# The output product of a gated MLP, taken for pairs of token tiles: seven block products in place of eight

## The chip, the core and the metric

The kernel runs on one core of one Trainium2 chip. The metric is the device time of one execution in microseconds. The program is one launch; nothing is computed on the host but the layout of the inputs.

The engines are named as in the profile: PE multiplies matrices (PEld is its loading of weights), DVE is the vector engine, ACT the scalar engine, POOL the general one, SP issues the DMAs. Matmul results land in banks of PSUM of 128 partitions x 512 float32 numbers, which DVE and ACT read. All other tiles are in SBUF.

## The reference

The input `x` has 2048 tokens of 512 numbers. It goes through a block of linear attention and then through a gated MLP, each behind a layer norm and a modulation by a condition `c`. Only the MLP matters here:

```python
z = gelu(h @ w_in)                    # h: 2048 x 512, z: 2048 x 1376
z1 = z[..., :688]
z2 = layernorm(z[..., 688:])
g = w_sp @ z2 + b_sp[:, None]         # w_sp: 2048 x 2048, mixes tokens
x = x + gb * ((z1 * g) @ w_out)       # w_out: 688 x 512
```

The change is in the last line: u = z1 * g, and u @ w_out with the gate `gb` already multiplied into `w_out`.

## The kernel before

Tokens lie in 16 tiles of 128, features on the free axis. Precision is kept by splitting each float32 operand into a high part, the copy to `fp32r` that ACT makes, and a low part, the rest, that DVE (sometimes POOL) subtracts. A product takes three matmuls, hi x hi, hi x lo and lo x hi, added up in one bank.

The program's order is written out by hand in lists of two-letter steps with arguments (`ORDER` for the first part, `ORDER3` for the rest); `run_all` emits them one after the other. Each engine, and SP for the DMAs, runs its own instructions strictly in this order; waits between engines come from the tiles that the steps write and read. `SLOTS` gives, tag by tag, the buffer number that each new tile takes: a tile's first write waits until the last reader of the tile before it in that buffer is done. `st` has 4 buffers of 4 KB a partition (raw pieces of `w_sp`, later the tiles `ur`), `s4` has 8, `md` 4, `zs` 16, `tq` 24.

`ORDER` does the attention and most of z. In `ORDER3` come, in this order:

- the token mixing g = w_sp @ z2. It is done for pairs of token tiles p = 0 to 7. The step `pr` is one of seven block products of a pair (pair 0 is done plainly by `pp`); `ss`, `fh`, `fl` and `fg` prepare the blocks of `w_sp`, and `cs`, `cd` and `ce` collect the banks P into u on DVE and ACT;
- for each tile t: `um` multiplies u by z1 (loaded by `lz`), `up` splits the words into two planes of 16 bits on ACT, `ux` transposes them by a DMA, `ug` merges them on ACT, `uq` parks the transposed u in DRAM. A transposed tile has six blocks of 128 columns: five with features 0 to 639, and a sixth whose partitions 0 to 47 and again 64 to 111 hold the last 48 features, so that one matmul over 112 partitions adds two of the three parts;
- the output product, PE's last stage. `ow`, `om`, `oh` and `os` load w_out in six blocks, multiply each by the gate and split it. For each tile, `ur` brings u back from DRAM into `st`, `uh` copies its high part on ACT (two instructions), `ul` makes the low part on DVE (three: L1039, L1041, L1042), `wm` does 17 matmuls into one bank `pout` (five blocks x 3, and 2 for the sixth), `ot` (L1086) adds the bank to the tile `x3` (loaded by `lx`) on DVE and stores it. The last tile is done in two halves of 256 columns, in two banks.

```python
PO[t, c0] = bank((t + (c0 > 0) + 7) % 8, f"pout{t}_{c0}")
...
mm3(p, v[:, 0], v[:, 1], WO[k][:, 0, c0:c1], WO[k][:, 1, c0:c1], k == 0, False)
```

Of the kernel before, what the change touches and what calls it, by code (L numbers as in the profile page):

```python
# [26 lines left out]
def block_kernel(ctx: ExitStack, tc: tile.TileContext, x, x_t, w_qkv, w_o, w_in, w_sp, b_sp, w_out,  # L27
# [3 lines left out]
    def pool(name, bufs, space=None, stack=None):  # L31
        if space is None:
# [28 lines left out]
        "tb": (
            "251640514236030560456512032560032302036043413024561031352613565461602135052644561533456312004154"
            "234246531320450302120102222300635564150423"
        ),
        "s4": (
            "106302405147035246037134521305131465713675741303537526703524167402671536504370142376454076531264"
            "315024517360017374267103627044167154073167540267503612751046237452601464563274610370567512037423"
            "20510673161562547073065123024513452134"
        ),
# [951 lines left out]
    UR = {}

    def u_back(t):
        UR[t] = sb("st", [P, 768], F32, f"ur{t}")
        dma(UR[t], UD[t])

# [159 lines left out]
```

## Time and profile before

| what | us |
|---|---|
| median of 3 runs | 617.71 (616.91 to 618.66) |
| the profiled execution's own time | 616.95 |
| its span, first to last instruction | 615.0 |
| busy in the span: PE | 608.7 |
| DVE | 464.2 |
| ACT | 362.2 |
| POOL | 212.2 |

The span is what the profile shows; the profiled execution took 1.95 us more. An engine is busy while it has an instruction in it, so PE's busy time tells that it is nearly always fed, not that it is at its peak. A line number is one of the kernel before; a helper such as `mm3` (L110 to L112) stands for all who call it, so tiles tell the stages apart: `pout<-wout,ut` is the output product. "x<-x,pout" is the output add, "ut<-ur,ut" the low part of u.

### The profile page before, as it was taken

The page shows a single profiled execution, that of the slowest core. Times are in us where ns is not written, and L with a number is a line of the kernel's source. Part 1 is how long each engine was busy: PE and PEld are TensorE (multiplying, and loading weights), DVE is VectorE, ACT ScalarE, POOL GpSimd, SP SyncE. Part 2 cuts the span into 40 slices and gives each one's busy share as a digit, 9 for nine tenths or more (in the row PEclk, how much of TensorE's full clock was granted, in tenths as well). Part 3 has the DMA queues.
Part 4 walks back from the last instruction along what each step waited for, and adds up shares of the span by engine and source line. Part 5 has one row for each costly group of instructions (what it writes and reads, how often), then busy time and mean ns, then how long its engine had stood idle before and what let it go on. Part 6 is the DMA issues. An engine that isn't in the chain of part 4 may idle for free.

```text
span 615.0 us, 9440 instructions
## 1 busy us (share of the span) xinstructions
PE 608.7 (99%) x3359; PEld 555.6 (90%) x3359; DVE 464.2 (75%) x873; ACT 362.2 (59%) x619; POOL 212.2 (34%) x180
## 2 busy tenths in 40 slices
...
GB/s 303 126 179 98 122 118 44 147 165 40 87 109 120 185 147 192 136 170 260 274 59 326 270 148 169 126 195 101 192 208 129 229 140 175 196 243 284 311 239 113
DMA packets 91022, 105.74 MB, mean 172 GB/s; under 512 B 57088, under 2 KB 57600, under 8 KB 90976
## 3 DMA queue, kind: packets, MB, share of 16 engines
...
q8 instruction: 26, 0.43, 0.3%
q14 instruction: 20, 0.16, 0.1%
...
## 4 chain that ended last, share of the span: by engine, by line
PE 84%; DVE 7%; ACT 3%; DMA 3%; POOL 1%; issue 1%; SPq 1%; ACTq 0%; DVEq 0%; POOLq 0%
PE P L944 30%; PE z L654 13%; PE Pq L944 5%; PE z L860 2%; PE g L112 2%; PE g L110 2%; PE pout L112 2%; PE g L111 2%; PE pout L110 2%; PE pout L111 2%; PE qp L111 2%; PE qp L110 2%; PE qp L112 2%; PE kp L110 2%; PE kp L111 2%; PE kp L112 2%
## 5 line engine op out<-in xcount | busy, mean ns | idle before, releaser
L944 PE MATMUL P<-z,f 128*128 128x344 f32 x672 | 109.8, 320 | 0.0
L654 PE MATMUL z<-win,ht 128*128 128x344 f32 x672 | 107.9, 320 | 0.2 <-ACT z L659 0.2
L654 PEld LDWEIGHTS z<-win,ht 128*128 128x128 f32 x672 | 106.4, 188 | 1.3 <-ACT z L659 0.5
L944 PEld LDWEIGHTS P<-z,f 128*128 128x128 f32 x672 | 106.6, 188 | 0.0
L934 POOL TENSOR_TENSOR f<-raw_wsp,f 128x512 fp32r<-128x512 f32 x28 | 39.6, 1423 | 172.7 <-ACT f L931 150.2
L254 POOL TENSOR_TENSOR mv<-ve,mhalf 128x1 f32<-128x1 f32 x48 | 35.2, 736 | 68.3 <-DVE nm L387 34.4
L931 ACT ACTIVATE f<-raw_wsp 128x512 fp32r<-128x512 f32 x56 | 34.2, 626 | 37.2 <-PE P L944 20.3
L934 DVE TENSOR_TENSOR f<-sa,f 128x512 fp32r<-128x512 f32 x42 | 32.0, 769 | 18.5 <-ACT f L931 16.5
L931 ACT ACTIVATE f<-sa 128x512 fp32r<-128x512 f32 x42 | 25.8, 625 | 20.6 <-issue 8.4
L278 ACT COPY uca<-ucb 128x768 uint16<-128x768 uint16 x32 | 31.9, 1063 | 7.0 <-DMA ucb<-uca 6.9
L112 PE MATMUL pout<-wout,ut 128*128 128x512 f32 (+1 forms) x85 | 32.3, 380 | 0.7 <-DVE ut L1039 0.7
L110 PE MATMUL pout<-wout,ut 128*128 128x512 f32 (+1 forms) x85 | 32.5, 383 | 0.0
L111 PE MATMUL pout<-wout,ut 128*128 128x512 f32 (+1 forms) x85 | 32.2, 379 | 0.0
L1033 ACT ACTIVATE ut<-ur 128x384 fp32r<-128x384 f32 x32 | 15.6, 519 | 27.9 <-DMA ur<-ud 11.0
L944 PE MATMUL Pq<-z,wsp 128*128 128x344 f32 x192 | 31.0, 321 | 0.0
L944 PEld LDWEIGHTS Pq<-z,wsp 128*128 128x128 f32 x192 | 30.6, 188 | 0.0
L476 POOL TENSOR_TENSOR pksum<-pksum,tk 128x512 f32<-128x512 f32 x15 | 22.3, 1486 | 18.0 <-DVE tk L448 14.5
L268 ACT COPY uca<-us 128x768 uint16<-128x768 uint16 x32 | 24.9, 826 | 5.2 <-PE P L944 2.0
L583 POOL TENSOR_TENSOR prod<-pq,zrep 128x512 f32<-128x512 f32 x16 | 21.8, 1376 | 15.7 <-DVE den L591 5.0
L934 DVE TENSOR_TENSOR f<-raw_wsp,f 128x512 fp32r<-128x512 f32 x28 | 19.8, 714 | 8.3 <-ACT f L931 8.3
L112 PE MATMUL po<-m,pt 128*128 128x512 f32 x64 | 25.4, 397 | 0.1
L110 PE MATMUL po<-m,pt 128*128 128x512 f32 x64 | 25.4, 396 | 0.0
(254 smaller groups left out, 1546.4 us busy)
## 6 DMA issues: line engine op xcount, KB each, us to landing
...
```

The source lines that it names most:

```text
L110: mm(o, a_hi, b_hi, start=first, stop=False, **kw)
L111: mm(o, a_hi, b_lo, start=False, stop=False, **kw)
L112: mm(o, a_lo, b_hi, start=False, stop=last, **kw)
L254: nc.gpsimd.tensor_tensor(mv[:, 1:2], ve, mhalf, op=OP.pow)
L268: nc.scalar.copy(pl[:, h], v[:, :, h])
L278: copy(o[:, :, h], plt[:, h * n:(h + 1) * n].rearrange("p a b -> p (a b)"))
L476: nc.gpsimd.tensor_add(pksum, pksum, PK[t])
L583: nc.gpsimd.tensor_mul(pr, PQ[t], KV["z"])
L654: mm(p[:, b, :HB], a[:, i, kc], win[h][:, j, kc, b * HB:(b + 1) * HB], start=kc == 0 and k == 0, stop=kc == KC - 1 and k == 2)
L931: nc.scalar.activation(SF[p, h, k][:, 0], s_src(p, h, k), AF.Copy)
L934: eng.tensor_sub(SF[p, h, k][:, 1], s_src(p, h, k), f(SF[p, h, k][:, 0]))
L944: mm(B[key][:, :HB], a[:, x_], b[:, y_], start=i == 1, stop=i == n)
```

## The change

The features 0 to 511 of u and all 512 columns of w_out are cut in blocks of 256, and two token tiles 2p and 2p+1 are taken together. With A11, A12 the two feature blocks of tile 2p, A21, A22 those of tile 2p+1, and B11 to B22 the blocks of w_out, the product of 2 x 2 blocks is formed from seven block products in place of eight (Winograd's form). Each product is 128 tokens x 256 features x 256 columns, so 2 x 3 matmuls of 256 columns. The other 176 features (blocks 4 and 5 of the transposed tile) are multiplied as before, in 256-column halves.

New steps: `ua` forms one of four sums of blocks of u in place in the returned tiles (DVE, 256 wide); `uH` and `uL` split the fourth, which needs a buffer of its own in `tq`; `wa` forms one of four sums of blocks of w_out (DVE); `op` is one block product, `or` one remaining half; `oa` adds a bank, or half of one, to `x3` (DVE). The tile `ur` grows from 768 to 1024 columns, so `uh` and `ul` cover 4 blocks a half instead of 3. w_out has nine split forms instead of six.

A pair has two banks. Half 0 of the first collects the products 1, 6, 7 and 4, one after the other; between them `oa` reads what is there, since M1, M1+M6 and M1+M6+M7 are needed by other blocks of the output. Its half 1 takes the rest of tile 2p+1. The second bank collects product 2 and the rest in one half, 5, 3 and the rest in the other.

Both orders and all of `SLOTS` are written anew. `ORDER` holds the same 836 steps in another sequence. `ORDER3` differs by the new steps too. Below stand the functions, the lines of the old order with most of `wm`, and the end of the new order.

```diff
-    UR = {}
+    UR, U4 = {}, {}
 
     def u_back(t):
-        UR[t] = sb("st", [P, 768], F32, f"ur{t}")
-        dma(UR[t], UD[t])
+        UR[t] = sb("st", [P, 1024], F32, f"ur{t}")
+        dma(UR[t][:, 256:], UD[t])
+
+    def u_sum(p, k):
+        a, b = UR[2 * p], UR[2 * p + 1]
+        a11, a12, a21, a22 = a[:, 256:512], a[:, 512:768], b[:, 256:512], b[:, 512:768]
+        if k == 3:
+            nc.vector.tensor_sub(a[:, :256], a11, a21)
+        elif k == 1:
+            nc.vector.tensor_add(a21, a21, a22)
+        elif k == 2:
+            nc.vector.tensor_sub(b[:, :256], a21, a11)
+        else:
+            nc.vector.tensor_sub(b[:, :256], a12, b[:, :256])
 
     def u_word(t, n):
-        return UR[t].rearrange("p (a b) -> p a b", b=P)[:, 3 * n:3 * n + 3]
+        return UR[t].rearrange("p (a b) -> p a b", b=P)[:, 4 * n:4 * n + 4]
 
     def u_hi(t):
         for n in range(2):
-            UT[t, n] = sb("s4", [P, 2, 3, P], F32R, f"ut{n}_{t}")
+            UT[t, n] = sb("s4", [P, 2, 4, P], F32R, f"ut{n}_{t}")
             nc.scalar.activation(UT[t, n][:, 0], u_word(t, n), AF.Copy)
 
     def u_lo(t):
@@ -1038,13 +1053,39 @@
             if n == 0:
                 nc.vector.tensor_sub(o[:, 1], v, f(o[:, 0]))
             else:
-                nc.vector.tensor_sub(o[:, 1, :2], v[:, :2], f(o[:, 0, :2]))
-                nc.vector.tensor_sub(o[64:112, 0, 2], v[64:112, 2], f(o[64:112, 0, 2]))
-
-    WO = {}
+                nc.vector.tensor_sub(o[:, 1, :3], v[:, :3], f(o[:, 0, :3]))
+                nc.vector.tensor_sub(o[64:112, 0, 3], v[64:112, 3], f(o[64:112, 0, 3]))
+
+    def u4_src(p):
+        return u_word(2 * p + 1, 0)[:, :2]
+
+    def u4_hi(p):
+        U4[p] = sb("tq", [P, 2, 2, P], F32R, f"u4_{p}")
+        nc.scalar.activation(U4[p][:, 0], u4_src(p), AF.Copy)
+
+    def u4_lo(p):
+        nc.vector.tensor_sub(U4[p][:, 1], u4_src(p), f(U4[p][:, 0]))
+
+    def u_form(p, k, i):
+        if k == 3:
+            return U4[p][:, :, i]
+        a, b = 2 * p, 2 * p + 1
+        t, n = {1: (a, 0), 2: (a, 2), 4: (b, 2), 5: (b, 0), 6: (b, -2), 7: (a, -2)}[k]
+        n += 2 + i
+        return UT[t, n // 4][:, :, n % 4]
+
+    def u_rest(t, k):
+        return UT[t, 1][:, :, k - 2]
+
+    WR, WO = {}, {}
 
     def load_wout(k):
-        r = RAW["wout", k] = sb("md", [P, D], F32, f"wor{k}")
+        if k < 4:
+            if k % 2 == 0:
+                WR[k // 2] = sb("st", [P, 2, D], F32, f"wor{k}")
+            dma(WR[k // 2][:, k % 2], w_out[k])
+            return
+        r = WR[k] = sb("md", [P, D], F32, f"wor{k}")
         if k < 5:
             dma(r, w_out[k])
         else:
@@ -1053,38 +1094,80 @@
             dma(r[64:112, :], w_out_tail)
 
     def wout_mul(k):
-        r = RAW["wout", k]
-        nc.vector.tensor_mul(r, r, MOD[5])
+        r = WR[k]
+        if k < 2:
+            nc.vector.tensor_mul(r, r, MOD[5][:, None, :].to_broadcast([P, 2, D]))
+        else:
+            nc.vector.tensor_mul(r, r, MOD[5])
+
+    def wout_sum(k):
+        b11, b12, b21, b22 = WR[0][:, :, :256], WR[0][:, :, 256:], WR[1][:, :, :256], WR[1][:, :, 256:]
+        if k == 1:
+            WR["t1"] = sb("md", [P, 2, 256], F32, "wt1")
+            nc.vector.tensor_sub(WR["t1"], b12, b11)
+        elif k == 2:
+            WR["t2"] = sb("md", [P, 2, 256], F32, "wt2")
+            nc.vector.tensor_sub(WR["t2"], b22, WR["t1"])
+        elif k == 3:
+            nc.vector.tensor_sub(b12, b22, b12)
+        else:
+            nc.vector.tensor_sub(WR["t2"], b21, WR["t2"])
+
+    def w_form(k):
+        return {1: lambda: WR[0][:, :, :256], 2: lambda: WR[1][:, :, :256], 3: lambda: WR[1][:, :, 256:],
+                4: lambda: WR["t2"], 5: lambda: WR["t1"], 6: lambda: WR["t2"], 7: lambda: WR[0][:, :, 256:],
+                8: lambda: WR[4].rearrange("p (a b) -> p a b", b=256),
+                9: lambda: WR[5].rearrange("p (a b) -> p a b", b=256)}[k]()
 
     def wout_hi(k):
-        WO[k] = sb("zs", [P, 2, D], F32R, f"wout{k}")
-        nc.scalar.activation(WO[k][:, 0], RAW["wout", k], AF.Copy)
+        WO[k] = sb("zs", [P, 2, 2, 256], F32R, f"wout{k}")
+        nc.scalar.activation(WO[k][:, 0], w_form(k), AF.Copy)
 
     def wout_lo(k):
-        nc.vector.tensor_sub(WO[k][:, 1], RAW.pop(("wout", k)), f(WO[k][:, 0]))
-        if k == 5:
-            nc.gpsimd.memset(f(WO[k][64:P, 1, :]), 0.0)
+        nc.vector.tensor_sub(WO[k][:, 1], w_form(k), f(WO[k][:, 0]))
+        if k == 9:
+            nc.gpsimd.memset(f(WO[9][64:P, 1]), 0.0)
 
     def load_x3(t):
         X3[t] = sb("tq", [P, D], F32, f"x3_{t}")
         dma(X3[t], X1D[t])
 
-    PO = {}
-
-    def wout_mm(t, c0=0, c1=D):
-        PO[t, c0] = bank((t + (c0 > 0) + 7) % 8, f"pout{t}_{c0}")
-        p = PO[t, c0][:, c0:c1]
-        for k in range(5):
-            v = UT[t, k // 3][:, :, k % 3]
-            mm3(p, v[:, 0], v[:, 1], WO[k][:, 0, c0:c1], WO[k][:, 1, c0:c1], k == 0, False)
-        v = UT[t, 1][:112, 0, 2]
-        mm(p, v, WO[5][:112, 0, c0:c1], start=False, stop=False)
-        mm(p, v, WO[5][:112, 1, c0:c1], start=False, stop=True)
-
-    def out_store(t, c0=0, c1=D):
-        o = X3[t][:, c0:c1]
-        nc.vector.tensor_add(o, o, PO[t, c0][:, c0:c1])
-        dma(out[t * P:(t + 1) * P, c0:c1], o)
+    PO, NPO = {}, {}
+
+    def o_bank(p, b, c):
+        if (p, b) not in PO:
+            PO[p, b] = bank((2 * p + 7 + b) % 8, f"pout{p}_{b}")
+        return PO[p, b][:, 256 * c:256 * c + 256]
+
+    def o_mm(p, b, c, a, w, last):
+        k = p, b
+        NPO[k] = NPO.get(k, 0) + 1
+        mm(o_bank(p, b, c), a, w, start=NPO[k] == 1, stop=last, skip_group_check=True)
+
+    def o_prod(p, k):
+        b, c = {1: (0, 0), 6: (0, 0), 7: (0, 0), 4: (0, 0), 2: (1, 0), 5: (1, 1), 3: (1, 1)}[k]
+        for i in range(2):
+            v = u_form(p, k, i)
+            for x_, y_ in ((0, 0), (0, 1), (1, 0)):
+                o_mm(p, b, c, v[:, x_], WO[k][:, y_, i], i == 1 and x_ == 1)
+
+    def o_rest(p, n):
+        b, c = ((1, 0), (1, 1), (0, 0), (0, 1))[n]
+        t, h = 2 * p + n // 2, n % 2
+        v = u_rest(t, 4)
+        for x_, y_ in ((0, 0), (0, 1), (1, 0)):
+            o_mm(p, b, c, v[:, x_], WO[8][:, y_, h], False)
+        v = u_rest(t, 5)[:112, 0]
+        for y_ in range(2):
+            o_mm(p, b, c, v, WO[9][:112, y_, h], y_ == 1)
+
+    def o_add(p, n):
+        t, b, c0, c1, k = ((0, 0, 0, 256, 0), (0, 0, 256, 512, 0), (1, 1, 256, 512, 256), (1, 0, 256, 512, 0),
+                           (1, 0, 0, 256, 0), (1, 0, 256, 512, 256), (1, 0, 0, 512, 0), (0, 1, 0, 512, 0))[n]
+        o = X3[2 * p + t][:, c0:c1]
+        nc.vector.tensor_add(o, o, PO[p, b][:, k:k + c1 - c0])
+        if n > 3:
+            dma(out[(2 * p + t) * P:(2 * p + t + 1) * P, c0:c1], o)
 
...
-        wm0 cs7,5 uq12 lx4 cd7,3 cd7,2 ul5 ul3 ur4 ug13 wm2 lx13 wm1 ot0 wm5 wm3 ur6 lx15 uh4 uh6 um14 ur8
-        lz15 cs7,0 uh7 uq13 lx3 ul4 ur10 ot1 wm4 ul6 up14 ot2 uh8 ur9 ul7 ot3 ur12 ot4 ux14 um15 wm7 ot5 ul8
-        uh10 wm6 lx8 wm8 uh9 ot6 up15 ul10 ur11 ug14 ot7 ux15 uq14 ur13 ul9 uh11 ot8 uh12 wm9 ur14 ul11 ug15
-        ul12 wm10 wm11 lx12 uh13 ot9 wm12 ul13 uq15 ot10 ur15 ot11 uh14 uh15 ot12 ul14 ul15 wm13 wm14
-        wm15,0,256 ot13 ot14 ot15,0,256 wm15,256,512 ot15,256,512
...
+        fg7,0,4 lx0 om4 pr7,0,3 wa2 fg7,1,2 lx4 ur1 pr7,0,5 oh8 ux13 cs7,5 pr7,1,7 os2 oh1 pr7,1,2 os1 oh6 os6
+        fh7,1,3 fl7,1,3 oh7 ur2 pr7,1,3 ug12 os7 cd7,2 oh5 wa4 ua0,3 uq12 oh3 pr7,0,4 cs7,7 cd7,3 um14 os8
+        ua0,1 uh0 pr7,1,4 up14 os3 ua0,2 ul0 op0,1 op0,2 ur3 cd7,4 oa0,0 uh1 or0,0 os5 ug13 ul1 ux14 ua0,4 oh4
+        ua1,3 op0,6 lx5 op0,5 lz15 oa0,1 ua1,1 op0,7 oa0,2 uH0 cs7,0 uL0 uh2 uq13 oa0,3 ur4 ul2 or0,1 op0,3
+        ur5 os4 ug14 uq14 or0,2 op1,1 ua1,2 uh3 op1,2 um15 up15 lx6 ul3 lx7 ua1,4 op0,4 oa1,0 lx10 or1,0 ua2,3
+        op1,5 or1,3 uH1 oa1,2 or0,3 ua2,1 ur6 ur7 uL1 op1,6 or1,1 ua2,2 op1,3 uh4 lx12 ux15 oa1,1 ul4 uh5
+        op1,7 ur9 ul5 ua2,4 oa1,3 oa0,7 uH2 op2,1 op2,2 ua3,3 or2,0 lx8 oa2,0 op2,5 or1,2 uh6 ur8 ug15 oa0,6
+        uL2 or2,3 op2,6 oa2,2 uq15 op1,4 ua3,1 op2,3 ul6 op3,1 lx13 ua3,2 oa2,1 oa1,7 op3,2 ur10 uh7 ur11
+        op2,7 or2,1 oa3,0 ul7 op3,6 ua3,4 op3,5 ua4,3 oa2,3 oa3,1 or3,3 or2,2 oa3,2 op3,7 ua4,1 uH3 uL3 op3,3
+        uh8 oa1,6 or3,1 oa2,7 ua4,2 uh9 ul8 ul9 ur13 op2,4 op4,1 lx15 ur12 or3,0 oa4,0 ua4,4 op4,2 uH4 oa3,3
+        ua5,3 op4,5 op4,6 oa4,2 oa2,6 uh10 or3,2 lx11 ua5,1 or4,3 ur15 uL4 oa4,1 ua5,2 op3,4 ul10 uh11 or4,1
+        ul11 or4,0 ua5,4 op4,7 ua6,3 op4,3 op5,2 op5,1 op5,5 oa3,7 oa4,3 ua6,1 oa5,0 oa5,2 uh12 or5,0 uH5 uL5
+        ul12 ur14 or4,2 oa3,6 ua6,2 op5,6 op4,4 op6,1 or5,1 op6,2 oa6,0 uh13 or6,0 oa4,7 ul13 oa5,1 ua6,4
+        op6,5 or5,3 lx14 oa6,2 uH6 op5,7 oa4,6 op5,3 ua7,3 oa5,3 ua7,1 op6,6 or6,3 op5,4 ua7,2 oa5,7 or6,1 uL6
+        uh14 or5,2 oa6,1 op6,3 uh15 ul14 oa5,6 op7,2 ul15 op6,7 ua7,4 op7,5 uH7 oa6,3 oa6,7 op7,1 op6,4 or6,2
+        uL7 oa7,0 op7,6 oa7,2 or7,0 oa6,6 op7,3 or7,1 oa7,1 op7,7 oa7,7 oa7,3 or7,3 or7,2 op7,4 oa7,5 oa7,4
```

More of the change, by code (lines that the diff above doesn't have):

```diff
@@ L60, in block_kernel @@
-        "pst": "01010100100110100",
+        "zs": "bd9fcbf08e40c26a1538e324ac8578a127c4ace8c147a8eca7e87a7e8a78ef239061cea7d485b3f6e920b1",
+        "md": "10013230131301013030101330310310330012",
+        "ta": "40352405143321051043310542150145230514342521553150424234501522341",
+        "s4": (
+            "634073365367410253016457547174171643721672163130724432741765234072605314371305026723416730416365"
+            "402421507264530627104103561725130657420754237631253463207716532240706247512306756402313427602437"
+            "56620341561734601521707234501276145102"
+        ),
@@ L61, in block_kernel @@
+        "pst": "00111001100100011",
+        "st": (
+            "231000013210121030213013013021320312012301203123013102233310230112032310312030210231301230123012"
+            "302130"
+        ),
         "tb": (
[L62 to L69 removed]
@@ L813, in block_kernel @@
-        wo5 q415 d115 hp3 hh2 hl2 ht1 d18 d27 he1 d26 x14 hm3 z12 z01 z02 g22 ap7 d19 h24 hh3 hl3 hp4 lX8 d28
-        g11 z13 d210 hm4 ap6 am7 x15 hh4 am6 hl4 lX10 h25 g12 ah6 al6 z11 g23 ah7 ap8 al7 z14 d29 hp5 d215
-        ap10 zl0 wo6 am8 wo7 lX7 z04 hm5 g24 ah8 d112 g21 d111 am10 al8 hh5 ap9 d212 g14 zl2 x17 zl4 lX6 lX9
-        ah10 hl5 zn2 am9 zn0 ah9 zp2 zh2 al9 wo8 h27 d211 z05 al10 hp7 x16 zn4 ap11 z03 zl1 zo2 h26 zp0 x18
-        d113 wo10 zn1 wo9 hp6 g15 zh0 x110 z15 hm7 hh7 g13 h28 ap12 hl7 d213 am11 g25 z17 hp8 ah11 x19 g27
@@ new lines, in block_kernel @@
+        lW1,2 d24 d17 x10 wh1,2 wl0,3 ae1 wo3 ae2 wo1 x13 w02 ap4 q214 h20 wl1,2 d25 ht0 he0 wl1,3 w12 q414
+        q215 x12 ap5 am4 ah4 h22 z00 al4 hp2 za0 wo4 lX4 x11 am5 ah5 al5 h23 g10 hm2 hh2 d16 h21 zb0 hp3 q415
+        lX7 lX5 wo5 hl2 ht1 d18 z12 d27 g20 d26 he1 x14 hm3 g22 ap6 d19 h24 z01 z02 hh3 hl3 hp4 d28 d115 x15
+        am6 hm4 ap7 z13 g11 g12 hh4 z11 am7 h25 d29 lX6 g23 ah7 ah6 hl4 al6 d210 z14 al7 hp5 d111 zl2 d215 wo6
+        z03 ap8 zl3 zl0 d112 g24 ap9 d211 ap10 lX8 hm5 lX9 g21 wo7 hh5 zn2 x16 am9 am8 ah8 zh2 am10 zo2 ah9
```

173 lines of the change are left out of this document (85 added, 88 removed).

## The prediction

> **What bounds the kernel now.** I read the page's busy times first, then the waits of PE, then PE's instructions in order of time through the last stage, then the busy time of every engine there.
>
> ```profile
> span 615.0 us, 9440 instructions
> ...
> PE 608.7 (99%) x3359; PEld 555.6 (90%) x3359; DVE 464.2 (75%) x873; ACT 362.2 (59%) x619; POOL 212.2 (34%) x180
> ```
> ```profile
> PE warm L172 <- POOL tiny L124: 1.0, 1, 1.0
> PE pout L112 <- DVE ut L1039: 0.7, 1, 0.7
> PE wm L332 <- ACT cbr L326: 0.7, 1, 0.7
> ```
>
> PE is busy for 608.7 of 615.0 us, and these three waits are the largest of six (the others 0.2 each): PE's instruction stream is the kernel. A shorter stream shortens the run, and every new wait of PE lengthens it one for one.
>
> ```profile
> 547.51 0.39 PE L110 MATMUL pout<-wout,ut 128*128 128x512 f32 x1
> ...
> 603.77 0.40 PE L110 MATMUL pout<-wout,ut 128*128 128x512 f32 x1
> ...
> 607.70 0.29 PE L110 MATMUL pout<-wout,ut 128*128 128x256 f32 x1
> ...
> 611.64 0.28 PE L1082 MATMUL pout<-wout,ut 112*128 112x256 f32 x1
> ```
>
> This is the stage that changes. The second column is the latency of one matmul; what counts is the distance of the starts. From 603.77 to 607.70 lie the 17 matmuls of tile 14, 512 columns wide: 0.231 us each. From 607.70 to 611.64 lie 33 steps of the two halves of tile 15, 256 columns wide, each with its own weight load: 0.1194 us each, 0.004 more than half of 0.231. The stage runs from 547.51 to 611.76, 64.25 us with the one wait of 0.7.
>
> ```profile
> 548.90:611.90 63.00, 62.28 (x284) 50.58 (x282) 31.99 (x69) 25.74 (x44) 0.52 (x1) 1.00 0.83 246
> 500.00:548.90 48.90, 48.90 (x310) 48.57 (x309) 35.95 (x61) 28.44 (x48) 8.36 (x6) 1.00 0.63 194
> ```
>
> After the length stand PE, PEld, DVE, ACT, POOL, the granted clock (1.00, so the clock has no part in this) and the DMA share. In the last stage DVE works 32 us of 63 and the DMA engines are 83% busy.
>
> **The change, part by part.** PE: a pair of tiles now takes 2 x 17 matmuls of 512 columns. After it takes 7 x 2 x 3 = 42 for the block products and 4 x 5 = 20 for the remaining 176 rows, all of 256 columns: 62 x 0.1194 = 7.40 us a pair, 59.2 for eight. Against 64.25 that is -5.0 us, if PE never waits.
>
> DVE gets more work, in narrower pieces:
>
> ```profile
> L1086 DVE TENSOR_TENSOR x<-x,pout 128x512 f32<-128x512 f32 x15 | 10.1, 686 | 6.2 <-PE pout L1082 6.0
> L1039 DVE TENSOR_TENSOR ut<-ur,ut 128x384 fp32r<-128x384 f32 x16 | 8.9, 556 | 16.9 <-ACT ut L1033 16.9
> L1041 DVE TENSOR_TENSOR ut<-ur,ut 128x256 fp32r<-128x256 f32 x16 | 6.7, 421 | 6.1 <-ACT ut L1033 6.0
> L1042 DVE TENSOR_TENSOR ut<-ur,ut 48x128 fp32r<-48x128 f32 x16 | 4.6, 290 | 0.4
> ```
> ```profile
> 574.75 0.29 DVE L1042 TENSOR_TENSOR ut<-ur,ut 48x128 fp32r<-48x128 f32 x1
> 575.07 1.29 DVE L1086 TENSOR_TENSOR x<-x,pout 128x512 f32<-128x512 f32 x2
> ...
> 577.65 0.55 DVE L1039 TENSOR_TENSOR ut<-ur,ut 128x384 fp32r<-128x384 f32 x1
> 578.12 0.42 DVE L1041 TENSOR_TENSOR ut<-ur,ut 128x256 fp32r<-128x256 f32 x1
> 578.57 0.29 DVE L1042 TENSOR_TENSOR ut<-ur,ut 48x128 fp32r<-48x128 f32 x1
> ```
> ```profile
> 367.41 0.50 DVE L903 TENSOR_TENSOR t_5r<-o,t_5r 128x344 fp32r<-128x344 f32 x1
> 367.84 0.50 DVE L903 TENSOR_TENSOR t_3r<-o,t_3r 128x344 fp32r<-128x344 f32 x1
> ```
>
> In a full queue the next instruction starts before the last one ends: two adds of 512 take 1.29, so the second starts 0.60 after the first; 384 wide takes 0.47 of the queue, 344 wide 0.43. The line through them gives 0.34 for 256 (an estimate; alone it takes 0.42). The 48x128 piece overlaps neither side: 0.32, and what stands before it takes its whole duration and 0.03. So per pair, after: the sums ua 4 x 0.34; the split ul 2 x (0.60 + 0.58 + 0.32) = 3.0; uL 0.34; the output adds 4 x 0.34 + 2 x 0.60. Together 7.3 us, against PE's 7.40. Before it was 2 x 1.24 + 2 x 0.60 = 3.7 against 7.9. This is the point of the case: DVE, half idle in this stage before, becomes as long as PE, and PE now waits for it both ways, because after each of the products 1, 6 and 7 (op) an add (oa) must read the partial sum out of the bank before the next may be added to it.
>
> How far DVE falls behind can be counted in the new order, whose end is printed above. I put PE's first product op0,1 at 0. DVE is in order, and oa0,0 can't start before op0,1 has ended: 0.72, 0.16 for the last matmul's latency and 0.04 to the reader, 0.9 us, and I take 0.1 for the way back to PE (an estimate). From oa0,0 through oa5,2 the list holds 50 pieces of 256, 7 adds of 512, 11 ul, 2 wout splits, one um of 0.79 and one cs of 0.5: 17.0 + 4.2 + 16.5 + 1.2 + 1.3 = 40.2 us. PE's product or5,0 writes the bank that oa5,2 reads, and PE's work ahead of it is 37 op and 19 or, 317 x 0.1194 = 37.8. So 0.9 + 40.2 + 0.1 - 37.8 = 3.4 us of waiting by there, even if DVE itself never waits. Counted in the same way, ul13 ahead of op6,5 gives 2.4 and ul4 ahead of op2,1 0.9. Before shows no matmul into one half of a bank while the other half is read (the halves of tile 15 lie in two banks), so whether or5,0 must wait for the other half's reader is open: 2.4 if not, 3.4 if so. I take 3.4, because the code makes the bank one tile of 512 columns, and keep 2.4 for the range.
>
> The Trainium skill, PSUM — Partial Sum Buffer, section "PSUM bank collisions raise a hardware error", speaks against sharing a bank: a PE write and a VectorE read in one bank at once are an error even at other columns, and the rule is to guard by bank. By it the term is 3.4, without it 2.4; no run here shows it yet.
>
> DVE's own waits come on top:
>
> ```profile
> L1033 ACT ACTIVATE ut<-ur 128x384 fp32r<-128x384 f32 x32 | 15.6, 519 | 27.9 <-DMA ur<-ud 11.0 <-PE pout L112 5.9 <-DMA x<-x1d 3.4
> L278 ACT COPY uca<-ucb 128x768 uint16<-128x768 uint16 x8 | 7.9, 1054 | 2.8 <-DMA ucb<-uca 2.8
> ```
> ```profile
> ucb<-uca SPq DMA_TRANSPOSE x4, 5.0
> ```
> ```profile
> L1025 SPq DMA_DIRECT2D ur<-ud x16: 319/368/627, 523.4 to 598.8; - x16
> ...
> DMA to landing us min/median/max: 3.3/4.7/6.5
> ```
>
> The last two rows are those of the returns ur: 0.4 us to issue, 4.7 to land. Two places. First, ux14 stands in the list where PE is at 2.0; its transpose lands 5.0 later, ug14 takes ACT 2 x 1.05 from there, and uh3 queues behind it to about 10.2, where DVE wants to finish ul3 from 9.4: some 0.3 us. Second, ur12 takes over the buffer that uL4 reads last (33.9 in DVE's count, 34.8 on the clock), is issued 0.4 and lands 4.7 later, near 39.9, where DVE wants it at 38.8: 1.0 us. Together 1.3. The other late returns come in time by the same count: ur7 (18.1 against 18.0), ur11 (32.4 against 32.8), ur14 (46.5 against 47.9).
>
> ```profile
> 611.96 0.42 DVE L1086 TENSOR_TENSOR x<-x,pout 128x256 f32<-128x256 f32 x1 [1.60 <-PE pout L1082]
> ```
>
> At the very end or7,3, or7,2 and op7,4 all go into the bank that oa7,3 reads, and oa7,3 waits for op7,7: PE stands 0.16 + 0.04 + 0.42, 0.6 us. After the last matmul two adds and two stores follow where one did: +0.4.
>
> The rest I cost at nothing, with its cover. The w_out forms: 6 x 2 x 0.60 = 7.2 us of DVE before; after, two gatings of 1024 (1.13, the same line), two of 512, four sums and nine splits, 11.3. The 4.1 more lie in the 48.9 us ahead of the stage, where DVE is idle for 13; without that cover op0,1 comes up to 4.1 late. ACT's splits of 512 instead of 384 cost some 32 x 0.11 and uH 8 x 0.4 (estimates from 0.52 for 384), 7 us in a stage where ACT is idle for 37. DMA: the same loads, transposes, parks, returns and stores in number and bytes; the two widest w_out pieces now sit in two of the four st buffers, so ur3 waits for their last reader (os3, ahead of op0,1) and lands about when DVE asks for it. SP is in order: its stores wait for the adds of each pair with later returns queued behind them, which is part of the DMA rival below. The first order holds the same 836 entries rearranged; it can win back at most the 1.3 us of waits other than the first and the stage's own, and I allow as much loss, zero in the sum.
>
> **The sum.** The profiled execution took 616.95 us: 616.95 - 64.25 + 59.2 + 0.4 + (3.4 + 1.3 + 0.6) = 617.6. It lies 0.76 below the median 617.71 of the runs, so the runs should show 618.4. In short, 613.1 plus PE's waits in the stage, here 5.3. Of this kernel 0.3% (1.85 us) is about what can be told from no change: faster needs under 2.75 us of waits, slower over 6.45.
>
> **The rivals.** *The wide bank tile holds nothing up.* If only the half that is read is guarded, the lead is 2.4; if the 1.3 is covered and the last stand goes as well (or7,3 runs under oa7,3), waits are 2.4 and the time is 615.5, faster. For it: all of DVE's 58.1 us after oa0,0 are less than PE's 59.2. Against it: DVE may then idle no more than some 2% of the stage, and in the profile it sits 23 us waiting for ACT's ut. It decides at 2.75.
>
> *Returns land late.* Before, ACT waited 11.0 us for ur, with DMA at 83%. At 6.5 instead of 4.7, ur7, ur11 and ur12 come 1.8 later each, and DVE has nothing to give back: two of them add 3.6, 622.0; all three 623.8.
>
> *Narrow pieces don't overlap.* If every DVE instruction takes its whole duration (0.42, 0.69; ul 1.59), the same count peaks at 10.3 ahead of op7,6: 613.1 + 10.3 + 1.3 + 0.6 = 625.3. Against it: the spacings of 0.60 and 0.43 quoted. The Trainium skill, VectorE: DVE Perf Modes, section "The DRAIN you can't avoid", says that the next operation starts only when the pipe has emptied, which would be this rival; the rows of 512 and 344 columns disagree.
>
> *The matmuls don't get shorter.* Above 0.1295 a piece (64.25 / 496) nothing is saved on PE. The last 34 matmuls, with as many weight loads, run at 0.1194, so this is nearly out.
>
> **How the numbers follow.** The forecast, waits of 3.4 to 6.4 and hence 616.5 to 619.5, gets 0.46: within 0.3%. The guarded half gets 0.17, and it is all of faster. Late returns get 0.25, no overlap 0.07, and 0.05 is left for costlier matmuls and a worse first order: slower 0.37. The range 614.8 to 623.0 takes in the first rival with 0.7 us to spare for the first order, and two late returns with 1 us; it leaves out no overlap and three late returns.
>
> **What will show it.** Right: 496 pout matmuls at 0.119 in steps; DVE busy over 60 us of the last 65 where it was 32; PE's waits in the stage 3 to 6 us in many small pieces, put down to DVE's x (oa) and ut, the largest single ones near or5,0 and at or7,3. Wrong: PE without waits there and a time under 616 (the reads cost less than counted); DVE idle behind ACT's ut and DMA's ur for over 5 us (the returns); or PE's waits ahead of 547, which would be the first order or the w_out sums.

## The result, and the profile after

The changed kernel takes 623.84 us (median of 6 runs, 622.25 to 624.78) against 617.08 for the kernel before on the same chip: 1.0103 times as long, 95% interval 1.0084 to 1.0122. It is slower by 6.8 us, more than the 0.3% that counts as no change, and 0.8 us above the range given. The profiled execution took 623.89 us with a span of 622.1, which is 7.1 more than before.

The first view is PE's waits, of which before had three of any size: engine and line, what it waited for, us in total, times, the longest.

```profile
PE pout L1145 <- DVE x L1168: 3.8, 6, 1.1
PE pout L1145 <- DVE ut L1054: 1.7, 2, 1.1
PE pout L1145 <- ACT ut L1048: 1.0, 2, 0.8
...
PE P L947 <- DVE c L982: 0.9, 1, 0.9
...
PE po L113 <- DVE xr L633: 0.7, 1, 0.7
PE P L947 <- DVE f L937: 0.4, 1, 0.4
PE pm L115 <- DVE kvh L131: 0.3, 1, 0.3
```

In the output product PE now stops ten times, and in the token mixing ahead of it (`P<-`) twice where it never stopped. The waits for xr and kvh, in the attention, are new too. The second view is PE in order of time: the rows that begin behind a stop, the number in brackets being its length, and one long row without a stop.

```profile
550.32 0.50 PE L1145 MATMUL pout<-wout,ut 128*128 128x256 f32 x2 [0.23 <-ACT ut L1048]
551.93 2.43 PE L1145 MATMUL pout<-wout,ut 128*128 128x256 f32 x17 [1.11 <-DVE ut L1054]
555.00 1.44 PE L1145 MATMUL pout<-wout,ut 128*128 128x256 f32 x10 [0.64 <-DVE ut L1054]
556.89 1.57 PE L1145 MATMUL pout<-wout,ut 128*128 128x256 f32 x11 [0.45 <-DVE x L1168]
...
564.23 2.73 PE L1145 MATMUL pout<-wout,ut 128*128 128x256 f32 x21 [0.91 <-DVE x L1168]
...
572.23 2.28 PE L1145 MATMUL pout<-wout,ut 128*128 128x256 f32 x17 [0.50 <-DVE x L1168]
...
580.11 2.13 PE L1145 MATMUL pout<-wout,ut 128*128 128x256 f32 x16 [0.76 <-ACT ut L1048]
...
584.82 6.73 PE L1145 MATMUL pout<-wout,ut 128*128 128x256 f32 x55
...
595.55 6.24 PE L1145 MATMUL pout<-wout,ut 128*128 128x256 f32 x50 [1.14 <-DVE x L1168]
602.09 1.58 PE L1145 MATMUL pout<-wout,ut 128*128 128x256 f32 x11 [0.30 <-DVE x L1168]
...
616.28 2.18 PE L1145 MATMUL pout<-wout,ut 128*128 128x256 f32 x16 [0.51 <-DVE x L1168]
```

The 55 matmuls from 584.82 take 6.73 with the last one's latency, so the spacing is 0.119 to 0.12, as forecast. The stage begins at 550.32 instead of 547.51. It ends at 618.30, 0.12 past the start of the last matmul, so it is 67.98 us long where it was 64.25. Take 496 x 0.1194 = 59.2 away and 8.8 us of waiting are left: 6.55 in the ten brackets, the rest in restarts (the first matmuls behind a stop start further apart, 0.2 us or so in all each time) and small gaps.

The third view is the busy time of each engine in the stage and in the 50 us ahead of it, with the columns shown before:

```profile
550.32:618.42 68.10, 61.78 (x496) 59.73 (x496) 60.36 (x141) 30.40 (x51) 0.00 (x0) 1.00 0.69 207
500.00:550.32 50.32, 50.09 (x319) 49.81 (x318) 42.31 (x66) 33.83 (x57) 12.72 (x9) 1.00 0.78 221
```

DVE is busy 60.36 of 68.10 us where it was 32 of 63. So the loss has three places: 2.8 us before the stage starts, 3.7 in the stage (5.05 won by PE, 8.8 waited), and 0.5 for the second add and store behind the last matmul (3.79 us from there to the end of the span, 3.28 before).

### The profile page after: what moved, and what is told of

Same layout as the page of the kernel before. It is cut to its first block, busy times and chain, and to the rows that moved or that the text cites. A ratio compares the mean times of both kernels' runs of the same rounds, so it can differ in the third digit from the quotient of the medians.

```text
span 622.1 us, 9993 instructions
## 1 busy us (share of the span) xinstructions
PE 607.8 (98%) x3566; PEld 563.7 (91%) x3566; DVE 510.3 (82%) x950; ACT 370.8 (60%) x630; POOL 220.0 (35%) x180
## 4 chain that ended last, share of the span: by engine, by line
PE 84%; DVE 8%; ACT 2%; DMA 2%; issue 2%; SPq 1%; DVEq 0%; POOL 0%; ACTq 0%; POOLq 0%
PE P L947 23%; PE z L657 16%; PE pout L1145 6%; PE Pq L947 5%; PE z L863 2%; PE po L113 2%; PE po L115 2%; PE po L114 2%; PE qp L113 2%; PE g L113 2%; PE qp L115 2%; PE qp L114 2%; PE g L114 2%; PE g L115 2%; PE kp L115 2%; PE kp L113 2%
## 5 line engine op out<-in xcount | busy, mean ns | idle before, releaser
L937 POOL TENSOR_TENSOR f<-raw_wsp,f 128x512 fp32r<-128x512 f32 x28 | 41.5, 1490 | 171.3 <-ACT f L934 156.7
L257 POOL TENSOR_TENSOR mv<-ve,mhalf 128x1 f32<-128x1 f32 x48 | 38.9, 813 | 77.7 <-DVE ve L256 39.8
L1145 PE MATMUL pout<-wout,ut 128*128 128x256 f32 (+1 forms) x448 | 57.5, 284 | 6.6 <-DVE x L1168 3.8
L1145 PEld LDWEIGHTS pout<-wout,ut 128*128 128x128 f32 (+1 forms) x448 | 54.6, 189 | 8.7 <-DVE x L1168 3.2
L937 DVE TENSOR_TENSOR f<-sa,f 128x512 fp32r<-128x512 f32 x42 | 34.1, 818 | 21.1 <-ACT f L934 21.0
L1048 ACT ACTIVATE ut<-ur 128x512 fp32r<-128x512 f32 x32 | 19.0, 626 | 19.2 <-PE pout L1145 11.8
L1168 DVE TENSOR_TENSOR x<-x,pout 128x256 f32<-128x256 f32 (+1 forms) x49 | 23.1, 497 | 6.4 <-PE pout L1145 6.2
L113 PE MATMUL qp<-wq,ht 128*128 128x512 f32 x64 | 25.4, 396 | 0.0
```

The source lines that it names most:

```text
L113: mm(o, a_hi, b_hi, start=first, stop=False, **kw)
L257: nc.gpsimd.tensor_tensor(mv[:, 1:2], ve, mhalf, op=OP.pow)
L937: eng.tensor_sub(SF[p, h, k][:, 1], s_src(p, h, k), f(SF[p, h, k][:, 0]))
L1145: mm(o_bank(p, b, c), a, w, start=NPO[k] == 1, stop=last, skip_group_check=True)
L1168: nc.vector.tensor_add(o, o, PO[p, b][:, k:k + c1 - c0])
```

## The experiments

Sixteen kernels were timed against the kernel before on the same chip. "Excess" is the median less that of the kernel before timed beside it. "Mixing" runs from the first matmul of the token mixing to the first of the output product (185.09 before), "stage" is the output product (64.25 before); both come from one profiled execution. In three runs that execution also lost 2 to 4 us ahead of the mixing, outside both columns: the first matmul of the mixing stands at 367.06 in "old first order", 366.45 in "adds kept, bank not read" and 365.07 in "all repairs", and at 362.4 to 364.0 in all others.

| run | excess, us | ratio, 95% interval | mixing | stage |
|---|---|---|---|---|
| the change | 6.76 | 1.0103 (1.0084 to 1.0122) | 187.38 | 67.98 |
| old first order | 10.55 | 1.0161 (1.0143 to 1.0179) | 187.97 | 67.6 |
| new first order, old product | 1.05 | 1.0024 (1.0012 to 1.0035) | 186.10 | 64.13 |
| no partial reads | 0.12 | 1.0005 (0.9996 to 1.0014) | 187.19 | 61.31 |
| adds kept, bank not read | 2.90 | 1.0054 (1.0034 to 1.0073) | 187.28 | 63.47 |
| small piece left out | 2.65 | 1.0052 (1.0038 to 1.0066) | 186.99 | 63.90 |
| ur1 earlier | 4.92 | 1.0081 (1.0068 to 1.0094) | 187.08 | 66.74 |
| small piece on POOL | 4.85 | 1.0081 (1.0068 to 1.0095) | 187.30 | 65.91 |
| sixth block by a mask | 4.75 | 1.0077 (1.0059 to 1.0096) | 187.28 | 65.81 |
| three low parts on DVE | 6.04 | 1.0104 (1.0090 to 1.0117) | 186.77 | 68.0 |
| four low parts on DVE | 11.19 | 1.0182 (1.0164 to 1.0199) | 191.03 | 68.0 |
| three repairs | 7.65 | 1.0123 (1.0104 to 1.0142) | 190.96 | 64.6 |
| three repairs, ul0 first | 9.27 | 1.0149 (1.0130 to 1.0168) | 190.98 | 66.3 |
| or5,0 later | 6.57 | 1.0100 (1.0087 to 1.0113) | 187.27 | 67.0 |
| four or steps later | 4.95 | 1.0076 (1.0063 to 1.0089) | 187.14 | 65.36 |
| moves, ur1, low parts | 2.27 | 1.0032 (1.0020 to 1.0044) | 185.82 | 64.42 |
| all repairs | -0.31 | 0.9991 (0.9980 to 1.0002) | 186.24 | 61.80 |

### Which order costs the time ahead of the stage

```diff
 old first order: ORDER of the kernel before, ORDER3 and product of the change
-    ORDER = """ (new list)
+    ORDER = """ (old list, with its buffers)
 new first order, old product: the reverse
```

> The first order of before (its 836 steps, with its buffer numbers), the second order and the product of after. Theory A (the loss lies in the output stage and in the second order just ahead of it, where DVE's in-order queue is full): the product's first matmul starts within 1 us of after's 550.3 and the time stays at 622.5 to 624.5, +0.9 to +1.2% on before. Rival B (the new first order costs the 2.8 us by which the stage starts later): 620.5 to 621.5, +0.6%, first matmul at 547.5 to 548.5.

> The new first order with the old second order and the old product of 512 columns. Theory 'the order ahead of the product is where 2.8 us go, and it is the second order': first P matmul near 363, first pout matmul near 548, time as before +0.2 to +0.8 us, 617.0 to 617.6. Rival 'the new first order costs it': +2 to +3 us, 619 to 620.

The first run came out as neither text had it and says little on the size: where the old list meets the new one, a stop of 2.3 us for z arises that neither kernel has.

```profile
331.12 9.40 PE L863 MATMUL z<-win,ht 128*128 128x344 f32 x48 [2.31 <-ACT z L869]
```

But the mixing is 0.6 longer than in the changed kernel (187.97 for 187.38), not shorter, so the 2.3 us by which it grew from the kernel before do not come from `ORDER`. The second run lies between the two expectations. Its own mixing is 1.0 longer than before, at two stops (368.23 and 378.65) where the lists meet and which neither kernel has, so its excess of 1.05 is no clean price of `ORDER`. In the changed kernel's trace `ORDER` costs 0.5, within the loss that the forecast had allowed, and the rest belongs to `ORDER3`.

### DVE's length, or the hand-over of the bank

`oa` with n up to 3 reads the partial sums M1, M1+M6 and M1+M6+M7 and the like. Three runs take away the reads with their DVE work, the reads alone, and DVE work alone. The first two do not add these partial sums to the output, the third leaves the low part of the last 48 features out.

```diff
 no partial reads
-        nc.vector.tensor_add(o, o, PO[p, b][:, k:k + c1 - c0])
+        if n > 3:
+            nc.vector.tensor_add(o, o, PO[p, b][:, k:k + c1 - c0])
 adds kept, bank not read
+        nc.vector.tensor_add(o, o, PO[p, b][:, k:k + c1 - c0] if n > 3 else o)
 small piece left out
-                nc.vector.tensor_sub(o[64:112, 0, 3], v[64:112, 3], f(o[64:112, 0, 3]))
```

> After without the adds oa 0 to 3 (the four 256-wide reads per pair of partial sums and of product 5; they are left out, so the output lacks these terms). It takes 32 x 0.34 = 10.9 us of work off DVE's queue in the stage and every hand-over from PE to DVE and back inside a pair. Theory A (DVE's queue is too long): PE's waits in the stage fall from 8 us to about 2 (those at its start), time 617 to 618.5, the same as before. Rival H (the hand-overs alone cost the waits): the same 617 to 618.5. It bounds what both can explain together; if waits stay above 5 us, both are wrong and the returns of u or ACT are the cause.

> After with the adds oa 0 to 3 kept at the same width on DVE, but adding the tile x3 to itself and reading no bank (so the output is another one). DVE's queue is as long as in after; no hand-over inside a pair is left. Theory A: DVE's own waits for PE (about 2 us) go, all else stays: 621 to 623.5. Rival H: waits fall to about 2 us, 617 to 618.5.

> After without the 48x128 piece of ul (16 instructions of DVE; its part of the low halves keeps the high value, so the output is slightly off). It takes 16 x (0.32 + 0.11) = 6.9 us off DVE's queue and leaves every hand-over. Theory A: PE's waits fall by 4 to 6 us, time 618 to 620. Rival H: within 1 us of after, 623 to 624.5.

The stage falls to 61.3, 63.5 and 63.9. By the times, the first run is at the edge of what both theories gave, the second lies between the two (619.73), and the third is what the long queue gave (619.48). So neither theory holds alone. With the same DVE work and no hand-over 4.5 us of the stage go, more than a long queue by itself would give; with all hand-overs and some 6.9 us less DVE work (by the spacings) 4.1 go, though a pure hand-over price would have stayed. The reading that fits all three is that a hand-over is paid for where DVE comes late to it.

### The late start

In the changed kernel DVE comes to the stage late. Its instructions in order of time, a few of them:

```profile
547.16 0.43 DVE L1034 TENSOR_TENSOR ur<-ur,ur 128x256 f32<-128x256 f32 x1 [1.52 <-DMA ur<-ud]
...
548.52 0.88 DVE L1001 TENSOR_TENSOR us<-us,z1r 128x688 f32<-128x688 f32 x1
549.32 0.69 DVE L1127 TENSOR_TENSOR wout<-wor,wout 128x512 fp32r<-128x512 f32 x1
...
550.26 0.69 DVE L1127 TENSOR_TENSOR wout<-wor,wout 128x512 fp32r<-128x512 f32 x1
...
551.19 0.68 DVE L1054 TENSOR_TENSOR ut<-ur,ut 128x512 fp32r<-128x512 f32 x1
...
553.33 0.41 DVE L1168 TENSOR_TENSOR x<-x,pout 128x256 f32<-128x256 f32 x1
```

ua0,3 waits 1.52 for ur1, and um14 and two splits of w_out (L1127) stand ahead of ul0 (L1054), for which PE stops 1.11 at 551.93.

```diff
-        ... um13 lx2 om1 ur0 ... fg7,0,4 lx0 om4 pr7,0,3 wa2 fg7,1,2 lx4 ur1
+        ... um13 om1 ur0 ... fg7,0,4 om4 pr7,0,3 wa2 fg7,1,2 ur1 lx2 lx0 lx4
```

> The steps lx2, lx0 and lx4 (three loads on SP's queue) stand behind ur1 instead of ahead of it, so that u's second tile is asked for about 1 us earlier. Theory 'the stage starts late because DVE waits 1.5 us for this return and carries it through the stage': DVE's wait in front of ua0,3 shrinks to 0.5 us or less, PE's two stops of 0.2 and 1.1 at op0,1 go, -1.0 to -1.5 us against the changed kernel, 622.3 to 622.9. Rival 'the late start is absorbed later, because DVE and PE wait for each other anyway': 0 to -0.3 us, 623.5 to 623.9.

The time is as the first theory had it. The stops at op0,1 go, and all later ones stay as they were to 0.01 us (0.64, 0.45, 0.91, 0.50, 0.76, 1.14, 0.30, 0.51). The stage is 1.24 shorter: this much of the late start is paid in full and nothing later gives it back. The first add oa0,0 now starts 1.83 after op0,1 instead of 3.01.

### Fewer DVE instructions with the whole output computed

```diff
 small piece on POOL
-                nc.vector.tensor_sub(o[64:112, 0, 3], v[64:112, 3], f(o[64:112, 0, 3]))
+                nc.gpsimd.tensor_sub(o[64:112, 0, 3], v[64:112, 3], f(o[64:112, 0, 3]))
 sixth block by a mask (tail is 0 on partitions 0 to 63, 1 on the others)
+            nc.scalar.activation(UT[t, 1][:, 0, 3], u_word(t, 1)[:, 3], AF.Copy, scale=tail)
 ...
-                nc.vector.tensor_sub(o[:, 1, :3], v[:, :3], f(o[:, 0, :3]))
-                nc.vector.tensor_sub(o[64:112, 0, 3], v[64:112, 3], f(o[64:112, 0, 3]))
+                nc.vector.tensor_sub(o[:, 1], v, f(o[:, 0]))
```

> The 48x128 piece of ul goes from DVE to POOL, which has nothing else to do in the stage; all is computed. Theory 'DVE's queue is too long': 6.9 us less on DVE as in the run that left the piece out, so 619.5 to 620.5. Rival 'POOL's two-input instructions hold DVE's as they did in the P stage (0.7 us stretched to 1.7)': each of the 16 pieces stops DVE for 0.3 to 0.5 us or more and gives back what DVE won, 623 to 626.

> The 48x128 piece of ul disappears with nothing left out: ACT copies the high part of the sixth block with a scale of 0 on partitions 0 to 63 and 1 on the others, so that one subtraction of 512 gives the rounded value on the first partitions and the low part on the others. DVE 16 x (0.58 + 0.32 - 0.60) = 4.8 us less, ACT 16 instructions of 128 columns more (some 4 to 5 us). Theory 'DVE full, and made to wait by the hand-overs': as in the run that left the piece out, 619.3 to 620.2. Rival 'ACT's longer split now holds ul': 622 to 624, with DVE idle behind ACT's ut.

Both win about 2 us and miss their first expectation. The groups of DVE by line and form in the stage show why: of the changed kernel first, then with the piece on POOL, then with the mask.

```profile
L1168 DVE TENSOR_TENSOR x<-x,pout 128x256 f32<-128x256 f32 x32 | 12.9, 415 | 2.2 <-PE pout L1145 2.0
L1054 DVE TENSOR_TENSOR ut<-ur,ut 128x512 fp32r<-128x512 f32 x16 | 11.0, 686 | 0.1
L1168 DVE TENSOR_TENSOR x<-x,pout 128x512 f32<-128x512 f32 x15 | 10.1, 682 | 2.0 <-PE pout L1145 1.9
L1056 DVE TENSOR_TENSOR ut<-ur,ut 128x384 fp32r<-128x384 f32 x16 | 8.8, 552 | 0.6 <-ACT ut L1048 0.5
```

```profile
L1168 DVE TENSOR_TENSOR x<-x,pout 128x256 f32<-128x256 f32 x32 | 12.9, 411 | 2.9 <-PE pout L1145 2.8
L1054 DVE TENSOR_TENSOR ut<-ur,ut 128x512 fp32r<-128x512 f32 x16 | 12.5, 782 | 0.0
L1056 DVE TENSOR_TENSOR ut<-ur,ut 128x384 fp32r<-128x384 f32 x16 | 10.2, 635 | 0.6 <-ACT ut L1048 0.6
```

```profile
L1059 DVE TENSOR_TENSOR ut<-ur,ut 128x512 fp32r<-128x512 f32 x32 | 21.0, 686 | 1.4 <-ACT ut L1054 1.1
L1170 DVE TENSOR_TENSOR x<-x,pout 128x256 f32<-128x256 f32 x32 | 13.0, 415 | 2.9 <-PE pout L1147 2.7
L1170 DVE TENSOR_TENSOR x<-x,pout 128x512 f32<-128x512 f32 x15 | 10.1, 681 | 2.3 <-PE pout L1147 2.3
```

With the piece on POOL, the two subtractions of ul grow by 2.9 us in all (782 and 635 ns for 686 and 552), while the adds that read a bank (L1168) do not. With the mask there is no such loss, DVE has some 4.8 us less to do (by the spacings), and yet the stage falls by 2.2 only: DVE's idle time ahead of its adds, in the last column, grows from 4.2 us to 5.2, and that behind ACT from 0.7 to 1.4. A part of what DVE gains it spends waiting for PE, which waits for it.

### What PE waits for at the stops

All six stops from 564 on stand at a step `or`: or1,3, or2,3, or3,3, or5,0, or5,3 and or7,3, counted in PE's list. Each writes one half of a bank while an `oa` that reads the other half is still due. (The one at or3,3 is put down to ACT's ut in the changed kernel, but the add oa3,1 ends at 579.97, 0.14 ahead of it, as oa1,0 ends 0.15 ahead of or1,3; in the runs with less work on DVE it is put down to DVE's x.)

```diff
 or5,0 later
-        oa5,0 oa5,2 uh12 or5,0 uH5 uL5 ul12 ur14 or4,2 oa3,6 ua6,2 op5,6 op4,4 op6,1 or5,1
+        oa5,0 oa5,2 uh12 uH5 uL5 ul12 ur14 or4,2 oa3,6 ua6,2 op5,6 op4,4 op6,1 or5,0 or5,1
 four or steps later: this one, and
-        op1,5 or1,3 uH1 ... op1,6 or1,1          -  oa3,1 or3,3 or2,2 oa3,2 op3,7
+        op1,5 uH1 ... op1,6 or1,3 or1,1          +  oa3,1 or2,2 oa3,2 op3,7 or3,3
-        op7,3 or7,1 oa7,1 op7,7 oa7,7 oa7,3 or7,3
+        op7,3 oa7,1 op7,7 or7,1 oa7,3 oa7,7 or7,3
```

> One step of PE's list is moved: or5,0 (5 matmuls into half 0 of a bank) comes behind op6,1 instead of ahead of or4,2, so that it no longer follows the add oa5,2 that reads half 1 of the same bank. Theory 'the bank is held as a whole, and PE stops at the rest products that write the half not being read': PE's stop of 1.14 goes and none comes in its place, 1.1 to 1.5 us less than the changed kernel. Rival 'PE waits there because the next product needs DVE's work in any case': the stop moves to or4,2, op5,6 or op4,4 with 0.8 us or more, 0 to -0.4 us.

> Four such moves: or5,0 as before, or1,3 behind op1,6, or3,3 behind op3,7, and or7,1 (which writes the other bank) between op7,7 and the add that or7,3 has to wait for; oa7,7 behind oa7,3. Nothing else differs. Bank theory: the stops of 0.91, 0.76, 1.14 and 0.51 fall to 0.3, 0.2, 0 and 0, with 0.2 for each restart that goes: 2.8 to 3.4 us less than the changed kernel, 620.4 to 621. Rival 'the products themselves wait': 0 to -1.0, 622.8 to 623.8.

With or5,0 moved, the stop of 1.14 is gone and only 0.15 comes in its place, at or4,2; the stage is 1.0 shorter, a little less than expected, and the median, with its scatter, shows 0.2 to 0.6 of it. With four moves, PE's rows behind a stop from 564 on, and those without one:

```profile
564.25 2.17 PE L1145 MATMUL pout<-wout,ut 128*128 128x256 f32 x16 [0.22 <-DVE x L1168]
...
571.69 2.26 PE L1145 MATMUL pout<-wout,ut 128*128 128x256 f32 x17 [0.48 <-DVE x L1168]
...
579.15 2.18 PE L1145 MATMUL pout<-wout,ut 128*128 128x256 f32 x16 [0.35 <-DVE x L1168]
...
591.18 8.74 PE L1145 MATMUL pout<-wout,ut 128*128 128x256 f32 x68
600.15 1.58 PE L1145 MATMUL pout<-wout,ut 128*128 128x256 f32 x11 [0.23 <-DVE x L1168]
...
612.37 3.57 PE L1145 MATMUL pout<-wout,ut 128*128 128x256 f32 x27
```

0.91 became 0.22, 0.76 became 0.35, and those at or5,0 and or7,3 are gone but for the 0.15: 2.6 us of the stage without one instruction less. The time fell by 1.8 (excess) to 2.2 us (median), between the two expectations and short of the 2.8 to 3.4 that the bank theory gave. So these four waits were mostly not for a sum that PE needed, but for the other half of its bank. What is left of the first is op1,6, which follows 5 matmuls (0.6 us) earlier now and waits for its own partial sum; what is left of the second is or2,2, which adds to the half that oa2,3 reads. The code declares each bank as one tile, and no run declares its halves as two, so whether the wait comes from the tile or would be there for any use of one bank is not shown.

### The token mixing

Here DVE and POOL in order of time, in the changed kernel; the plain duration of such a DVE instruction is 0.69:

```profile
396.04 1.76 DVE L937 TENSOR_TENSOR f<-sa,f 128x512 fp32r<-128x512 f32 x1
...
415.03 1.78 DVE L937 TENSOR_TENSOR f<-sa,f 128x512 fp32r<-128x512 f32 x1
```

```profile
394.71 2.54 POOL L937 TENSOR_TENSOR f<-raw_wsp,f 128x512 fp32r<-128x512 f32 x2 [3.07 <-ACT f L934]
...
414.94 1.32 POOL L937 TENSOR_TENSOR f<-raw_wsp,f 128x512 fp32r<-128x512 f32 x1 [8.07 <-ACT f L934]
```

DVE's second one starts 0.09 behind POOL's and ends 0.55 after POOL's has ended (416.26): it stands still meanwhile. PE's two stops for f and c follow:

```profile
397.85 3.73 PE L947 MATMUL P<-z,f 128*128 128x344 f32 x22 [0.44 <-DVE f L937]
...
419.45 5.75 PE L947 MATMUL P<-z,f 128*128 128x344 f32 x35 [0.91 <-DVE c L982]
```

```diff
-        "fg": lambda p, h, k: s_lo(p, h, k, nc.gpsimd),
+        "fg": lambda p, h, k: s_lo(p, h, k, nc.vector if (p, h, k) in ((2, 1, 2), (2, 0, 2), (2, 1, 4)) else nc.gpsimd),
 four: and (3, 0, 2)
```

> Three low parts of w_sp's blocks (fg2,1,2, fg2,0,2 and fg2,1,4) go from POOL to DVE, 0.6 us each on DVE. Theory 'PE's two waits in the P stage come from DVE instructions of 1.7 us under POOL's': the rows of 1.66 to 1.78 at 396, 406 and 415 become 0.7, PE's waits of 0.9 and 0.4 for c and f shrink to 0.3 or less together, first P to first pout 186 instead of 187.4, 622.2 to 623. Rival 'DVE is simply full in this stretch by the new order': the waits stay or grow, 623.8 to 625.

> As the run with three low parts on DVE, and fg3,0,2 too: it is POOL's instruction at 414.3 that still stretched DVE's to 1.78 there, and in DVE's list it comes behind the sum c that PE waits for. Theory: DVE's row of 1.78 near 415 becomes 0.7, PE's wait of 1.3 for c falls to 0.3 or less, first P to first pout 185.5 to 185.9, time 622.3 to 622.8. Rival 'DVE is full there': the wait stays at 0.9 or more, 623.3 to 624.

With three, the stop for f is gone and the mixing is 0.6 shorter; the stop for c even grows (1.34), since POOL's instruction at 414.3 is still there, and the time lies between the two expectations. With the fourth, PE's rows are:

```profile
419.31 2.45 PE L947 MATMUL P<-z,f 128*128 128x344 f32 x14 [0.31 <-DVE c L982]
425.34 5.27 PE L947 MATMUL P<-z,f 128*128 128x344 f32 x22 [3.58 <-DVE f L937]
```

The stop for c fell to 0.31 as expected, but the total got 5 us worse, which neither expectation had: 3.58 of the new stop, and 1.7 of slower matmuls behind it (last section). On POOL this subtraction had run at 414; in DVE's list it stands behind um4, which waits 1.08 for a load, so PE got f late. The mechanism was right and the place wrong. Put right behind cs2,7, the four cost nothing of the kind: the mixing is 185.82 in "moves, ur1, low parts".

### Together

> Three edits together: the sixth block by a mask, ur1 ahead of the three loads lx, four low parts on DVE. If their gains add up (4.2 and 1.4 and 1.3 from 623.8): 616.9, the same as before. If they cover the same waits of PE: 618.5 to 619.5.

> The same three, and um14, os8 and os3 (0.8 + 0.6 + 0.6 us of DVE) stand behind ul0 instead of ahead of it. Theory 'PE's first stops in the stage come from these three in DVE's queue': the stops at op0,1 (0.2 and more) go, 0.3 to 0.8 less than the run with three repairs. Rival 'they only move the stop to ul1, the next that PE needs, and make u's tile 14 late': 0 to +0.7.

> The four moves, ur1 ahead of the three loads, and four low parts on DVE, the fourth (3,0,2) now right behind cs2,7, where PE does not yet wait for it. Sum of the single gains: 3.1 + 1.4 + 1.0 to 1.5 below the changed kernel, 618 to 618.5. If PE's stop for c of 0.9 stays or a new stop for f comes, 619 to 620.

> As the run before, and the sixth block by a mask (2.2 us less of the stage when alone, of which the four moves take a part). 616 to 617: just below or equal to the kernel before; over 618 if mask and moves remove the same stops.

The first two carry the misplaced fourth low part (stops of 3.4 for f, and slower matmuls behind them), which hides the rest and puts both outside what was expected; their stage of 64.6 shows mask and ur1 at work. Moving um14, os8 and os3 behind ul0 made it 1.7 longer, more than its rival allowed: ACT's up14 came behind um14 and held up uh1, for which PE stopped 1.04.

```diff
 moves, ur1, low parts = four or steps later + ur1 earlier + low parts of
-    ... cs2,0 fg3,0,2 fh3,0,4 ... cs2,7 um3
+    ... cs2,0 fh3,0,4 ... cs2,7 fl3,0,2 um3      (and the three of before on DVE)
 all repairs = the same + sixth block by a mask
```

Without the mask 618.97 us, half a us above the sum of the single gains, with it 616.39, as expected. That run's waits of PE in the output product are:

```profile
PE pout L1147 <- DVE x L1170: 0.7, 3, 0.3
...
PE pout L1147 <- DVE ut L1059: 0.3, 1, 0.3
```

The excess fell by 7.1 us; the single gains (1.8 for ur1, 1.8 for the moves, 2.0 for the mask, 0.7 for three low parts) make 6.3, and the fourth low part, which was never timed alone in its right place, comes on top. So the single gains about add up. The seven products are then worth as much as the eight: 616.39 against 616.70, ratio 0.9991 (0.9980 to 1.0002), which can't be told from no change. What the same repairs would give the kernel before was not run.

## Why the prediction was wrong

It forecast 617.6 for the profiled execution; 623.89 came, 6.3 more. By its own steps:

- *496 matmuls at 0.1194*: right, and so were DVE's spacings (pieces of 256 columns start 0.33 to 0.35 apart) and the end (0.5 for 0.4).
- *"The rest I cost at nothing, with its cover."* This failed first. The 13 us of idle DVE ahead of the stage were a sum over 48.9 us; the work of the w_out forms stands at the end of that stretch, behind a return that comes 1.52 late. The forecast had named what happens without cover ("op0,1 comes up to 4.1 late") and put its price at zero. The first add oa0,0 starts 3.01 after op0,1 (553.33 less 550.32), where 0.9 was counted: 2.1 us. The run with ur1 earlier wins 1.2 of it back; the rest is put down to um14 and the splits ahead of ul0, which the run that moved them did not separate.
- *The count through oa5,2.* From oa0,0's start to oa5,2's end DVE took 42.2 us where 40.2 and 1.3 of own waits were summed: 0.7 more. PE had waited 7.4 us by or5,0 instead of 4.7 (595.55 less 550.32, less 317 x 0.1194); this is the mis-sized term, and 2.1 of the 2.7 more is the late start. Behind or5,0 came 1.4 instead of 0.6, since the stop at or5,3 and the restarts had no term.
- *The bank is held as a whole*: right, at the very matmul named. The forecast gave it one place at 1.0 us and the last stand; PE stood so at six places, and moving the step at four of them won 2.6 us of the stage. That the hold can be avoided by another place of the same step was not seen.
- *The orders at zero*: this failed too. 2.8 us were lost ahead of the stage, 0.5 of it before the mixing. Of the other 2.3, two stops with their restarts make 1.7 and the one at 550.32 makes 0.4. POOL's holding of DVE was not reckoned with, since the forecast went by sums of idle time; the trace of before shows it as well:

```profile
413.98 1.29 POOL L934 TENSOR_TENSOR f<-raw_wsp,f 128x512 fp32r<-128x512 f32 x1 [7.64 <-ACT f L931]
...
414.11 1.71 DVE L915 TENSOR_TENSOR sa<-raw_wsp,raw_wsp 128x512 f32<-128x512 f32 x1
```

- *Late returns*: returns landed in 4.0 at the median; one of them, ur1, counted, by being asked for late. *Narrow pieces don't overlap*: out. The section that the forecast cites beside it (the Trainium skill, VectorE: DVE Perf Modes, "The DRAIN you can't avoid") adds itself that an operation that is not held starts earlier; the spacings above agree with that. *Half a bank free*: out for this code. The time of 623.8 that was given for three late returns came out by another way, so that it was met is chance.

In sum, of the 6.3 us that were missing, 2.8 lay ahead of the stage, 2.7 in the stage up to or5,0 and 0.8 in the rest of it.

Not settled: about 0.2 us of the mixing, and exactly where `ORDER` loses its 0.5 us before it. PE's waits there point to xr (0.7) and kvh (0.3), which the kernel before does not wait for, against three waits of 0.2 that it has and the changed kernel has not.
